# Turning float64 weights into float32 on the chip: another sign operation, one chunk cut in two, two products removed

## The chip, the cores and the metric

The kernel runs on one core of a Trainium2 chip. The metric is the device time of one execution in microseconds (us); the time before is the median of three runs, 744.95 us (744.57 to 745.61). The core has five engines that run their own instruction streams and wait for each other by semaphores: TensorE (PE, with its weight load PEld) multiplies matrices into PSUM, VectorE (DVE) and ScalarE (ACT) do elementwise work, GpSimd (POOL) does some copies, and SyncE (SP) issues DMA transfers. SBUF is the working memory, with 128 partitions.

## The reference

```python
# attention: 8 batches, 8 heads, 576 tokens, head width 64
kv  = einsum('bhsd,bhse->bhde', k, v)
out = einsum('bhsd,bhde->bhse', q, kv)
rms = sqrt(mean(out * out, axis=-1) + 1e-06)
x   = (out / rms * g_norm)          # regrouped to 4608 tokens x 512

# feed-forward: w1, w2 are 512 x 1024, w3 is 1024 x 1024, w_out is 1024 x 512
a = x @ w1
b = x @ w2
h = (a * b) @ w3
result = h @ w_out                  # 4608 x 512
```

The activations q, k, v come as float32. The four weights come as float64, and the chip's engines work on float32, so the kernel first has to turn eight bytes of each weight into four.

## The kernel before, in words

The work has a beginning and nine groups of 512 tokens. In the beginning the product of w3 and w_out is formed once (it depends on no token); afterwards each group of tokens is sent through the attention, the two gates a and b, and that folded matrix. The groups use a scheme with seven products in place of eight (`winograd`, line 709), whose sums are formed by DVE.

**The beginning.** w3 and w_out are cut into eight chunks of 128 columns of w3 (or rows of w_out). A chunk is one raw tile of 128 partitions x 1024 float64 values: 512 of the upper half of w3, then 512 of w_out, half a megabyte each. `load_next` (line 191) loads a chunk by two transfers, chunk 0 by four; there are four raw tiles, so the load of chunk 4 needs the raw tile of chunk 0 to be read out. Then, for each chunk c:

1. `conversion` (line 137) writes the 1024 float32 values to `chunks[:, c]`. It sees each float64 as two 32-bit words, `lo` and `hi`. ACT makes two passes: `low` (line 158), lo scaled by 2^-51 plus 2.0, which gives a number between 2 and 2 + 2^-19 whose last bits are the top bits of lo; and line 160, the absolute value of hi read as a float. DVE makes four steps: line 162 takes the sign bit from hi and puts it into `low`; line 166 clamps the absolute value; line 169 shifts it left by three; line 172 adds the two integers. The `yield`s cut this into ACT's first pass, ACT's second pass, and the DVE steps.
2. `turn_w3` (line 676): PE transposes the chunk's w3 part by four products with the identity (line 680), and ACT copies the result to SBUF (line 685).
3. `fold_chunk` (line 689): four products of 512 columns (line 693) add the chunk's share to the folded matrix. The first three stand before the turn of the next chunk, the fourth behind it.

`begin_next` (line 238) issues ACT's two passes of the next chunk, with a call of `between` between the two passes of every piece where it is given; `end_next` (line 247) issues the DVE steps and the next load. `conversions` (line 222) cuts a chunk into pieces, each a conversion of its own: chunk 0 into 256, 256 and 512 values, chunk 1 into 512 and 512, the others whole. The loop at line 1413 issues, for chunk c: the DVE steps of chunk c, three fold products, the turn of chunk c + 1, the fourth fold product. For c = 0 the turn of chunk 1 is passed as `between` to the conversion of chunk 2, so that ACT's copy of turned chunk 1 stands between ACT's two passes over chunk 2.

`keep_warm(n)` (line 271) issues n products of the identity with itself, which nobody reads. It is called with 14 before anything has landed, with 9 behind the turn of chunk 0, and with 2 behind the fourth fold product of chunk 0.

The upper half of w3 is followed by its lower half (four raw tiles, "b") and by w1 and w2 (eight raw tiles, "w"), converted in the same way: 20 raw tiles in all, the last of them in the first group of tokens, about 84 to 115 us from the start. The scratch `low` lies in a part of `ab` that is not yet in use; odd and even tiles take turns with it.

**Order of the work.** In the beginning the order on DVE, ACT and SP is as written; PE, POOL and SP have a written order throughout. Later a scheduler orders ACT and, in part, DVE by its own costs, so that a changed cost of one step can change the order of others.

Of the kernel before, what the change touches and what calls it, by code (L numbers as in the profile page):

```python
# [12 lines left out]
FP32 = mybir.dt.float32  # L13
U32 = mybir.dt.uint32
U16 = mybir.dt.uint16
I64 = mybir.dt.int64
AF = mybir.ActivationFunctionType
ALU = mybir.AluOpType
# [4 lines left out]
def kernel(  # L23
# [32 lines left out]
    nc = tc.nc  # L56
# [49 lines left out]
    def load_q_left(b):  # L106
# [20 lines left out]
    LEAST, MOST = (  # L127
        float(np.array(bits, np.uint32).view(np.float32)) for bits in (0x38000000, 0x47EFFFFF)
    )

    def scale_by(t, scale, by_scalar):
        if by_scalar:
            nc.scalar.activation(t, t, AF.Copy, scale=scale)
        else:
            nc.vector.tensor_scalar(out=t, in0=t, scalar1=scale, scalar2=None, op0=ALU.mult)

    def conversion(n, dst, raw, cols=slice(0, 1024), scale=None, by_scalar=False):

        dst, raw = (t if len(t.shape) == 3 else t[:, cols] for t in (dst, raw))
        if raw.dtype == FP32:  # L140
            yield
            yield
            nc.vector.tensor_copy(out=dst, in_=raw)
            if scale is not None:
                scale_by(dst, scale, by_scalar)
            return
        words = raw.bitcast(U32).rearrange("p (n w) -> p n w", w=2)
        lo, hi = words[:, :, 0], words[:, :, 1]

        low = ab[n % 2][:, NF // 2:].rearrange("p a i t -> p (a i t)")[:, cols]  # L150
        low_bits = low.bitcast(U32)
        if len(dst.shape) == 3:
            wide = dict(c=dst.shape[1])
            lo, hi, low, low_bits = (
                t.rearrange("p (c n) -> p c n", **wide) for t in (lo, hi, low, low_bits)
            )
        dst_bits = dst.bitcast(U32)
        nc.scalar.activation(low, lo, AF.Copy, scale=2.0 ** -51, bias=2.0)
        yield
        nc.scalar.activation(dst, hi.bitcast(FP32), AF.Abs)  # L160
        yield
        nc.vector.scalar_tensor_tensor(  # L162
            out=low_bits, in0=hi, scalar=0x80000000, in1=low_bits,
            op0=ALU.bitwise_and, op1=ALU.bitwise_or,
        )
        nc.vector.tensor_scalar(
            out=dst, in0=dst, scalar1=LEAST, scalar2=MOST, op0=ALU.max, op1=ALU.min
        )
        nc.vector.tensor_scalar(
            out=dst_bits, in0=dst_bits, scalar1=3, scalar2=None, op0=ALU.logical_shift_left  # L170
        )
        nc.vector.tensor_tensor(out=dst_bits, in0=dst_bits, in1=low_bits, op=ALU.add)  # L172
        yield
        if scale is not None:
            scale_by(dst, scale, by_scalar)
# [10 lines left out]
    raws = []  # L186
# [35 lines left out]
    def conversions(n):  # L222

        what, i = todo[n]
        if what == "w":
            dst = w_sb[:, i].rearrange("p w c f -> p (w c f)")

            return [conversion(n, dst, raws[n], scale=g_col, by_scalar=in_first_group)]
        if what == "b":
            return [conversion(n, chunks[:, 2 * i:2 * i + 2, 0, :], raws[n])]  # L230
        dst = chunks[:, i].rearrange("p w f -> p (w f)")
        cuts = [[0, 256, 512, 1024], [0, 512, 1024], [0, 1024]][min(i, 2)]
        return [conversion(n, dst, raws[n], slice(a, b)) for a, b in zip(cuts, cuts[1:])]

    begun = []
    in_first_group = False

    def begin_next(between=None):
        if len(begun) < len(todo):
            begun.append(conversions(len(begun)))  # L240
            for c in begun[-1]:
                next(c)
                if between is not None:
                    between()
                next(c)

# [24 lines left out]
    def keep_warm(n):  # L271

        t = bank(ps_mm, "mm")
        for _ in range(n):
            nc.tensor.matmul(t[:, 0:P], lhsT=ident, rhs=ident, start=True, stop=True)
# [1114 lines left out]
    with tc.manual_schedule(  # L1390
        engines={mybir.EngineType.DVE, mybir.EngineType.Activation, mybir.EngineType.SP}
    ):
        for _ in range(RAW):
            load_next()
        nc.scalar.activation(const.tile([P, 1], FP32, name="warm"), eps_col, AF.Sqrt)
        g_row = const.tile([1, P], FP32, name="g_row")
        for e in range(2):
            nc.scalar.dma_start(
                out=g_row[:, e * D:(e + 1) * D], in_=g_norm.rearrange("(o d) -> o d", o=1)
            )  # L1400


        keep_warm(14)
        begin_next()
        end_next()
        turn_w3(0, 0)
        keep_warm(9)
        begin_next()

        g_ps = bank(ps_at, "at")[:, 0:1]  # L1410
        nc.tensor.transpose(g_ps, g_row, ident[0:1, 0:1])
        nc.scalar.copy(g_col, g_ps)
        for c in range(KF):

            if c:
                begin_next()
            end_next()
            if c == 4:
                load_four("k", 0, 0)
                load_q(0, 0)  # L1420
            elif c == 5:
                load_four("v", 0, 0)
                load_q(0, 1)
                load_q_left(0)
            fold_chunk(0, c, range(NH - 1))
            if c == 0:
                begin_next(lambda: turn_w3(0, 1))
            else:
                turn_w3(*((0, c + 1) if c + 1 < KF else (1, 0)))
            fold_chunk(0, c, [NH - 1])  # L1430
            if c == 0:
                keep_warm(2)


        first = batch(0)
        first.start()
        BEGIN, PRODUCT = {1: 0, 4: 1}, {2: 0, 5: 1}
        norms = {}
        FIRST = len(converted) + KF - 1
        for c in range(KF):  # L1440
            if c in BEGIN:
                first.begin_q(2 * BEGIN[c], 2 * BEGIN[c] + 1)
                if c == max(BEGIN):
                    x_first = first.x_by_dma(0, nc.scalar.copy)
                    next(x_first)
                    next(x_first)
            if c - 1 in norms:
                all_of(norms[c - 1])
            if c < KF - 2:
                if c < max(BEGIN):  # L1450
                    begin_next()
                if c == max(BEGIN) + 1:
                    all_of(x_first)

                end_next(len(raws) < FIRST)
            elif c == KF - 2:
                run(sum_w(0))
            fold_chunk(1, c, [0])
            if c in BEGIN:
                first.begin_kv(BEGIN[c])  # L1460
                if c == max(BEGIN):
                    load_q_left(1)
            if c + 1 == KF:
                for r in range(2):
                    first.turn(2 + r)
                run(combine_x(0))
                end_next(False)
                for _ in range(3):
                    load_next()
            fold_chunk(1, c, range(1, NH - 1))  # L1470
            if c + 1 < KF:
                turn_w3(1, c + 1)
            if c in (max(BEGIN), KF - 2):
                begin_next()
            fold_chunk(1, c, [NH - 1])
            if c in PRODUCT:
                norms[c] = first.product(PRODUCT[c])
                next(norms[c])
                next(norms[c])
# [8 lines left out]
    for n, T in enumerate(groups):  # L1488
# [8 lines left out]
        def between():  # L1497
            while len(converted) < len(begun):
                with tc.issue_after(copies["u2"][-1].ins):
                    end_next()  # L1500
            next(pieces, lambda: None)()
            if T == FIRST_OF_TWO - 1 and p == 0:
                begun_p.append(True)
                if len(begun_p) == 2:
                    with tc.issue_after(adds["norm"].ins):
                        prepare_some(2)
            if T == FIRST_OF_TWO - 1 and p == 1 and len(prepared) < 3:
                with tc.issue_after(adds["c11" if len(prepared) > 1 else "c21"][-1].ins):
                    prepare_some(1)
            if T == 1 and p == 2 and not loaded_b:  # L1510
                for _ in range(3):
                    load_b()
            if T == FIRST_OF_TWO - 1 and p == 2:
                replaced.append(True)
                if len(replaced) == 2:
                    replace_a21()

        if T in IN_TWO:
            p = 2
# [130 lines left out]
```

## Time and profile before

| | |
|---|---|
| median of three runs | 744.95 us |
| the profiled execution | 744.86 us |
| its span, first to last instruction | 743.0 us |
| PE busy | 736.0 us |
| DVE busy | 629.7 us |
| ACT busy | 378.1 us |
| POOL busy | 21.8 us |
| sign step of the conversion (L162) | 23 instructions, 21.9 us in 18 of 1024 elements |
| products of `keep_warm` (L275) | 50 matrix instructions for 25 products |

One execution is recorded; the times are from the start of its span. "L162" is line 162 of the kernel. A group of the profile lists instructions of one line, engine and shape: their number, their busy time in us and the mean of one in ns, and then how long the engine was idle before them and what ended that. A float32 product shows as two matrix instructions. The chain of waits goes back from the last instruction, at each step to whatever released it; its shares tell which engine sets the time where. An engine can be busy all the time and set nothing, and one that is idle for a microsecond can set everything behind it. The granted clock is the share of TensorE's full clock that it was given.

### The profile page before, as it was taken

How to read it: one execution, taken by the hardware profiler on the slowest of the kernel's cores; microseconds unless marked ns; L12 is line 12 of the kernel's file. 1: busy time of each engine (PE TensorE's matmuls, PEld its weight loads, DVE VectorE, ACT ScalarE, POOL GpSimd, SP SyncE). 2: the span in 40 equal slices, each digit the busy share in tenths (PEclk: the TensorE clock that was granted, in tenths of full speed). 3: DMA queues.
4: the chain of work that ended last, by engine and by line, in shares of the span. 5: the costliest groups of instructions: out<-in, count | busy, mean ns of one | idle time of the engine just before them, and what ended most of it. 6: DMA issues, size and time to landing. Idle time of an engine off the chain costs nothing.

```text
span 743.0 us, 16815 instructions
## 1 busy us (share of the span) xinstructions
PE 736.0 (99%) x6843; PEld 658.6 (89%) x6843; DVE 629.7 (85%) x1233; ACT 378.1 (51%) x652; POOL 21.8 (3%) x29
## 2 busy tenths in 40 slices
PE   8999999999999999999999999999999999999998
PEld 5455788888899999999999999999999999999997
DVE  6987999967869689978996899689969987997797
ACT  6687777424652575257526752576277313212321
POOL 0000000132000000010000001000001000000000
PEclk9999999999999999999999999999999999999999
DMA  9996934599999698869886998598848662565454
GB/s 313 354 330 203 266 108 122 121 326 301 285 311 326 175 275 260 268 157 287 256 263 169 292 263 257 181 284 239 278 101 220 224 209 87 178 218 158 135 198 135
DMA packets 135456, 169.65 MB, mean 228 GB/s; under 512 B 78036, under 2 KB 110804, under 8 KB 135380
## 3 DMA queue, kind: packets, MB, share of 16 engines
q1 hardware_dynamic: 132928, 154.16, 68.8%
q10 hardware_dynamic: 2452, 14.42, 5.6%
q8 instruction: 54, 0.88, 0.5%
q14 instruction: 22, 0.18, 0.1%
HBM read 130.55 MB, written 20.71 MB: 204 GB/s over the span
## 4 chain that ended last, share of the span: by engine, by line
PE 96%; DVE 2%; ACT 1%; DMA 1%; issue 0%; SPq 0%; ACTq 0%
PE mm L723 36%; PE mm L1273 23%; PE mm L1015 21%; PE mm L693 7%; PE at L335 3%; PE at L723 2%; PE mm L413 1%; PE at L413 1%; PE at L680 1%; DMA raw<-in_moe_w_out_dram 1%; PE at L1316 0%; DVE ab L162 0%; PE at L432 0%; DVE c L896 0%; PE at L355 0%
## 5 line engine op out<-in xcount | busy, mean ns | idle before, releaser
L1064 ACT COPY slots<-mm 128x512 f32<-128x512 f32 x88 | 51.6, 586 | 125.9 <-PE mm L1273 83.1
L723 PE MATMUL mm<-xT,w_sb 128*128 128x256 f32 x448 | 102.9, 379 | 0.0
L723 PEld LDWEIGHTS mm<-xT,w_sb 128*128 128x128 f32 x448 | 84.4, 190 | 11.5 <-issue 0.5
L723 PE MATMUL mm<-xc,ws 128*128 128x256 f32 x336 | 76.1, 379 | 0.0
L723 PEld LDWEIGHTS mm<-xc,ws 128*128 128x128 f32 x336 | 63.8, 190 | 8.7
L741 ACT COPY slots<-mm 128x512 f32<-128x512 f32 x59 | 34.6, 586 | 69.1 <-PE mm L723 63.7
L693 PE MATMUL mm<-chunks,ab 128*128 128x512 f32 x128 | 60.7, 605 | 0.9 <-DVE chunks L172 0.9
L1068 DVE TENSOR_TENSOR slots<-mm,slots 128x512 f32<-128x512 f32 x66 | 45.1, 683 | 17.4 <-PE mm L1015 17.3
L1065 ACT COPY slots<-mm 128x384 f32<-128x384 f32 x88 | 42.3, 481 | 25.3 <-PE mm L1273 22.6
L1015 PE MATMUL mm<-ws,w3o_sb 128*128 128x128 f32 x350 | 53.9, 275 | 0.0
L381 DVE TENSOR_REDUCE inv<-sq 128x8 f32<-128x512 f32 (+1 forms) x40 | 24.6, 629 | 29.0 <-ACT sq L380 29.0
L1273 PE MATMUL mm<-w3o_sb,ab 128*128 128x128 f32 x368 | 48.9, 276 | 0.0
L1015 PEld LDWEIGHTS mm<-ws,w3o_sb 128*128 128x128 f32 x350 | 46.4, 192 | 0.0
L1273 PEld LDWEIGHTS mm<-w3o_sb,ab 128*128 128x128 f32 x368 | 45.4, 192 | 0.6
L1273 PE MATMUL mm<-w3o_sb,raw 128*128 128x128 f32 x340 | 43.5, 275 | 0.0
L693 PEld LDWEIGHTS mm<-chunks,ab 128*128 128x128 f32 x128 | 21.6, 190 | 22.6 <-issue 14.3
L1273 PEld LDWEIGHTS mm<-w3o_sb,raw 128*128 128x128 f32 x340 | 40.7, 192 | 0.0
L723 PE MATMUL mm<-xc,w_sb 128*128 128x256 f32 x160 | 38.5, 384 | 0.0
L723 PE MATMUL mm<-xT,ws 128*128 128x256 f32 x160 | 38.2, 382 | 0.1
L1069 DVE TENSOR_TENSOR slots<-mm,slots 128x384 f32<-128x384 f32 x66 | 36.4, 551 | 1.9 <-PE mm L1273 1.9
L308 ACT COPY xT<-xn 128x1024 uint16<-128x1024 uint16 x28 | 32.5, 1167 | 4.3 <-DMA xn<-xT 4.3
L723 PEld LDWEIGHTS mm<-xT,ws 128*128 128x128 f32 x160 | 30.1, 190 | 4.6 <-ACT slots L741 0.5
(243 smaller groups left out, 1649.0 us busy)
## 6 DMA issues: line engine op xcount, KB each, us to landing
w3o_sb<-w_l SPq DMA_DIRECT2D x21, 896.0 KB, 4.7
w3o_sb<-w3o_l SPq DMA_DIRECT2D x18, 896.0 KB, 6.7
raw<-in_moe_w_dram SPq DMA_DIRECT2D x31, 512.0 KB, 7.6
raw<-w3o_l SPq DMA_DIRECT2D x15, 896.0 KB, 4.7
w3o_sb<-w3o_l ACTq DMA_DIRECT2D x14, 896.0 KB, 4.6
k_sb<-in_k_dram SPq DMA_DIRECT2D x16, 576.0 KB, 5.1
v_sb<-in_v_dram SPq DMA_DIRECT2D x16, 576.0 KB, 6.3
q_sb<-in_q_dram SPq DMA_DIRECT2D x32, 256.0 KB, 4.0
```

The costliest lines, as they stand in the source:

```text
L308: copy(words(dst), src)
L335: nc.tensor.matmul(ps[r * D:(r + 1) * D, :], lhsT=k_sb[rows, r, cols], rhs=v_sb[rows, r, cols], start=(j == 0), stop=(j == JS - 1),)
L381: adds["norm"] = nc.vector.tensor_reduce(out=inv[:, i], in_=sq.rearrange("p (h d) -> p h d", d=D), axis=AX.X, op=ALU.add)
L693: nc.tensor.matmul(sums_ps[half][m], lhsT=w3T[half, c][:, m, :], rhs=chunks[:, c, 1, :], start=(c == 0), stop=(c == KF - 1),)
L723: nc.tensor.matmul(ps[:, u, :], lhsT=lhsT(a_name, u, c), rhs=rhs(b_name, c),  start=(u == 0 and c == 0 and new), stop=(c == chunks - 1), s ...
L741: copies.setdefault(name, []).append(nc.scalar.copy(t, ps))
L1015: nc.tensor.matmul(ps[place // 4][:, place % 4, :], lhsT=x, rhs=y, start=new and place // 4 not in seen, stop=True, skip_group_check=True,)
L1064: nc.scalar.copy(z[:, 0:4], ps[0])
L1065: return nc.scalar.copy(z[:, 4:7], ps[1][:, 0:3])
L1068: nc.vector.tensor_add(z[:, 0:4], ps[0], z[:, 0:4])
L1069: nc.vector.tensor_add(z[:, 4:7], ps[1][:, 0:3], z[:, 4:7])
L1273: nc.tensor.matmul(ps[place // 4][:, place % 4, :], lhsT=x[:, c, :], rhs=y[:, c, :], start=new and place // 4 not in seen, stop=(c == 1), ...
```

## The change

Four things are changed in the conversion and in the loop that calls it:

- The sign step has one input in place of two. The upper 16 bits of `low` are the same for every element (0x4000, as `low` lies between 2 and 2 + 2^-19). The new step reads the top 16 bits of each float64 (every fourth 16-bit element of the raw tile), keeps the sign bit, sets 0x4000, and writes the upper 16 bits of each element of `low` (every second 16-bit element).
- The passes and steps are kept in lists, and for the w_out piece of chunk 0 (`low_last`) their order is exchanged: ACT makes the absolute value first and `low` second, and DVE clamps and shifts first and takes the sign third.
- Chunk 2 is converted in two pieces of 512, w3 part and w_out part. `between` is called once per chunk, between the two passes of its last piece.
- The `keep_warm(2)` behind chunk 0 is gone.

```diff
+        low_top = low.bitcast(U16).rearrange("p (n w) -> p n w", w=2)[:, :, 1]
+        hi_top = raw.bitcast(U16).rearrange("p (n w) -> p n w", w=4)[:, :, 3]
...
-        nc.scalar.activation(low, lo, AF.Copy, scale=2.0 ** -51, bias=2.0)
-        yield
-        nc.scalar.activation(dst, hi.bitcast(FP32), AF.Abs)
-        yield
-        nc.vector.scalar_tensor_tensor(
-            out=low_bits, in0=hi, scalar=0x80000000, in1=low_bits,
-            op0=ALU.bitwise_and, op1=ALU.bitwise_or,
-        )
-        nc.vector.tensor_scalar(
-            out=dst, in0=dst, scalar1=LEAST, scalar2=MOST, op0=ALU.max, op1=ALU.min
-        )
-        nc.vector.tensor_scalar(
-            out=dst_bits, in0=dst_bits, scalar1=3, scalar2=None, op0=ALU.logical_shift_left
-        )
+        passes = [
+            lambda: nc.scalar.activation(low, lo, AF.Copy, scale=2.0 ** -51, bias=2.0),
+            lambda: nc.scalar.activation(dst, hi.bitcast(FP32), AF.Abs),
+        ]
+        steps = [
+            lambda: nc.vector.tensor_scalar(
+                out=low_top, in0=hi_top, scalar1=0x8000, scalar2=0x4000,
+                op0=ALU.bitwise_and, op1=ALU.bitwise_or,
+            ),
+            lambda: nc.vector.tensor_scalar(
+                out=dst, in0=dst, scalar1=LEAST, scalar2=MOST, op0=ALU.max, op1=ALU.min
+            ),
+            lambda: nc.vector.tensor_scalar(
+                out=dst_bits, in0=dst_bits, scalar1=3, scalar2=None, op0=ALU.logical_shift_left
+            ),
+        ]
+        if low_last:
+            passes, steps = passes[1:] + passes[:1], steps[1:] + steps[:1]
+        for f in passes:
+            f()
+            yield
+        for f in steps:
+            f()
         nc.vector.tensor_tensor(out=dst_bits, in0=dst_bits, in1=low_bits, op=ALU.add)
...
-        cuts = [[0, 256, 512, 1024], [0, 512, 1024], [0, 1024]][min(i, 2)]
-        return [conversion(n, dst, raws[n], slice(a, b)) for a, b in zip(cuts, cuts[1:])]
+        cuts = [[0, 256, 512, 1024], [0, 512, 1024], [0, 512, 1024], [0, 1024]][min(i, 3)]
+        return [
+            conversion(n, dst, raws[n], slice(a, b), low_last=i == 0 and a == 512)
+            for a, b in zip(cuts, cuts[1:])
+        ]
...
-                if between is not None:
+                if between is not None and c is begun[-1][-1]:
                     between()
...
-            if c == 0:
-                keep_warm(2)
```

## The prediction

> **What bounds the kernel now.** I read the busy shares and the chain on the page first, then the table of windows, then the chain of the first 25 us in order of time, then the rows of ScalarE (ACT) and VectorE (DVE) in those microseconds.
>
> ```profile
> PE 736.0 (99%) x6843; PEld 658.6 (89%) x6843; DVE 629.7 (85%) x1233; ACT 378.1 (51%) x652; POOL 21.8 (3%) x29
> ...
> PE 96%; DVE 2%; ACT 1%; DMA 1%; issue 0%; SPq 0%; ACTq 0%
> ```
>
> TensorE is busy for 736.0 of 743.0 us: only about 7 us in the whole run can be won by feeding it better. The windows say where these are:
>
> ```profile
> 9.00:18.58 9.58, 7.88 (x29) 3.96 (x28) 9.31 (x16) 7.58 (x11) 0.00 (x0) 1.00 1.06 380
> 18.58:42.59 24.01, 24.01 (x73) 11.03 (x74) 23.49 (x26) 16.82 (x20) 0.00 (x0) 1.00 1.05 353
> 83.34:130.00 46.66, 46.58 (x407) 40.42 (x406) 44.16 (x77) 35.73 (x58) 0.00 (x0) 1.00 0.48 133
> 130.00:735.00 605.00, 605.00 (x5875) 570.39 (x5874) 513.39 (x1057) 281.52 (x505) 21.10 (x23) 1.00 0.75 227
> ```
>
> Columns: stretch, length, busy time of PE, PEld, DVE, ACT, POOL, granted clock, DMA share, GB/s. PE misses 1.7 us between 9.00 and 18.58 and next to nothing from 18.58 to 735. What the change can win lies before 18.58, or a little later where new waits would appear. The chain there:
>
> ```profile
> 14.67 1.22 DVE ab L162
> 15.89 0.66 DVE chunks L166
> 16.57 0.70 DVE chunks L169
> 17.30 1.24 DVE chunks L172
> 18.54 0.04 issue
> 18.58 0.66 PE at L680 x4
> 19.24 3.52 PE mm L693 x8
> 22.75 0.44 PE at L680 x4
> ```
>
> The conversion of chunk 2 (four DVE steps of 1024 elements) ends at 18.54 and only then PE may turn it (L680). From there a chunk costs PE 4.00 us (turns of chunks 3, 4 and 5 start at 22.59, 26.55, 30.56) and DVE 3.73 us (L162 at 14.67, 18.44, 22.17), so PE is the bound. Whatever time PE has won at the turn of chunk 3, before 22.59, it keeps to the end, unless a later stage eats it.
>
> **The price of the new sign step.** The groups of the first 24 us:
>
> ```profile
> L162 DVE SCALAR_TENSOR_TENSOR ab<-raw,ab 128x1024 uint32<-128x1024 uint32 x3 | 3.7, 1219 | 0.0
> ...
> L162 DVE SCALAR_TENSOR_TENSOR ab<-raw,ab 128x512 uint32<-128x512 uint32 x3 | 2.1, 687 | 1.2 <-ACT ab L158 1.2
> L169 DVE TENSOR_SCALAR chunks<-chunks 128x1024 uint32<-128x1024 uint32 x2 | 1.4, 694 | 0.1
> L169 DVE TENSOR_SCALAR chunks<-chunks 128x512 uint32<-128x512 uint32 x3 | 1.3, 427 | 0.1
> ```
>
> The new step has one input, as L169 has: 0.69 us for 1024 elements and 0.43 for 512, against 1.22 and 0.69 of L162. It writes 2-byte elements with a gap, which no DVE row shows. Lower end 0.43 for 1024 (as if it ran like L169 at half the elements); upper end 1.22 (no gain over L162, which reads the same strided source). ACT's 16-bit strided copies (L294, L308: 1.05 to 1.18 us for 1024) cost no more than its 32-bit passes L158 and L160 (1.14 to 1.21), so the gap alone is no expense there. I take 0.69 and 0.43: same engine, same operation class, same count.
>
> The Trainium skill, VectorE: DVE Perf Modes, "What auto-detection actually checks", gives a one-source operation in SBUF two elements per cycle even with steps, and the fourfold rate only for 16-bit data of step 1; the trace shows the twofold rate at L169 alone. Against the change speaks Vector Engine (DVE) Microarchitecture Reference, "Measured stream behaviour on trn2": a port that hops every element costs 1.7 to 2.5 ns per column. By that an estimate is 1.0 to 1.4 us per 1024 (512 columns a port, 0.15 us fixed), and the sum below would become about 0.4 us won to 0.9 us lost; L162's source hops too and its 1219 ns equal L172's 1226 for the same words in one run, so at one element per cycle this trace shows no such cost.
>
> **The change step by step.** Pitches on DVE (start to start, same rows): a 512-step is followed after 0.45 us by one that needs its result and after its duration less 0.08 by one that does not (L162 at 10.41, L166 at 11.02); for 1024: 0.73 and duration less 0.09.
>
> 1. *Exchanged passes, chunk 0's w_out piece.* Its data come at 7.57 as now. Abs runs first, so the clamp starts at 8.28, shift 8.73, sign 9.07 (the low pass ends at 8.82), add 9.52 in place of 9.80. The first fold product moves from 10.64 to 10.36. Were the sign at its upper end, the add would start at 9.78: the exchange alone wins next to nothing.
>
> 2. *Chunk 1.* Two pieces of 0.34 + 0.45 + 0.46 + 0.61 = 1.86 in place of 2.13: DVE goes on at 13.86 in place of 14.67.
>
> 3. *Two unread products fewer.* They stand at 14.59, in PE's wait for ACT's copy of turned chunk 1 (14.13 to 14.72 now; 13.85 to 14.44 after, as its turn moves with the first product). Chunk 1's fold starts at about 14.60 in place of 15.04: 0.28 is step 1, 0.16 the products. PE then waits 0.27 us, less than the 0.89 and 0.80 it waits at 10.64 and 18.58 under a granted clock of 1.00, so I price the clock at nothing.
>
> 4. *Chunk 2 in two pieces.* DVE pays one set of fixed costs more (2 x 1.86 = 3.72, against 3.31 for one of 1024 with the new sign), but the turn needs the first piece alone, done at 15.80. PE turns chunk 2 after its three products, at 17.25 in place of 18.58. The second piece is done at 17.66. On ACT the first piece goes at 11.62 into idle time (idle from 11.61 to 13.05; chunk 2's w3 half has landed by then, as 1.4 us pass between landings), the second at 13.05; the copy of turned chunk 1 keeps its place before the last pass.
>
> 5. *What is late next: chunk 3.* Its data bound ACT, not the sign:
>
> ```profile
> 13.05 1.20 ACT L158 ACTIVATE ab<-raw 128x1024 f32<-128x1024 uint32 x1 [1.44 <-DMA raw<-in_moe_w_out_dram]
> 14.13 0.59 ACT L685 COPY ab<-at 128x512 f32<-128x512 f32 x1
> ...
> 15.84 1.17 ACT L158 ACTIVATE ab<-raw 128x1024 f32<-128x1024 uint32 x1
> 16.91 1.14 ACT L160 ACTIVATE chunks<-raw 128x1024 f32<-128x1024 f32 x1
> ```
>
> The trace's landing of chunk 3's last half is 15.73, so ACT's two passes cannot move and end at 18.05. The copy of turned chunk 2 comes behind them, 18.0 to 18.58, and chunk 2's fold can start at about 18.75, PE's own pace giving 18.62: 0.12 lost. DVE: sign of chunk 3 at 17.58, clamp 18.18 (it waits for ACT's 18.05), add 19.63, end 20.86. PE turns chunk 3 at about 21.35 in place of 22.59: **1.24 us won**, and DVE is half a microsecond ahead.
>
> 6. *Afterwards.* A chunk costs DVE about 3.2 us, PE 4.00; chunk 4 lands at 18.5 by the trace, ACT takes it up at 18.6 (19.75 now), chunk 5 at 21.3. DMA is full (share 1.05) but gains 1.2 us per chunk on PE. The load of chunk 4 is the one that waits for the sign's read: issued at 9.04 now, about 9.6 after, behind queues that are full until 15.73; nothing waits on SP's queue but the later loads. From 18.58 to 735 PE has no wait worth naming, except 0.24 us near 128.1 behind ACT's copy L741, whose row of ACT work starts from PE itself at 114.19 and moves with it. Some thirteen later signs save DVE 0.53 each; PE doesn't wait for them. The scheduler exchanges a few steps between 94 and 115 us: on ACT a scaling (L133, 1.14 us) gets ahead of a copy of a product (98.97); its bank is held until DVE's L896 at 106.00 in either case. Price nothing; if one such bank were awaited, 1.1 us.
>
> The sum: 744.86 of the profiled execution (span 743.0 and 1.86 around it) less 1.24 is 743.62; the median is 0.09 above that execution, so 743.7.
>
> **The rivals.**
> - *The sign gains nothing* (1.22 for 1024). Adds then end at 10.47, 14.73, 18.99 and 22.73 for chunks 0 to 3: chunk 2 in two pieces costs DVE 0.53, PE turns chunk 3 at 22.77. 0.18 lost: 745.1. For it: no such DVE row; against: L169. Between 0.82 and 1.22 the result slides from 743.7 to 745.1.
> - *More is won*: the wait near 128.1 (0.24) vanishes as DVE is relieved in 83 to 130 (44.16 of 46.66 busy): 743.4. Against: that chain is ACT's. A still faster sign wins nothing, because of chunk 3's landing.
> - *Slower*: the 2-byte gapped write costs DVE more than L162. Place: the seven half-steps up to chunk 3's add, then every chunk. From about 1.55 us for 1024 the run is slower by over 0.2%: the seven halves add 1.15 to the 0.18, and DVE's chunk exceeds PE's 4.00 from 1.49 on. At twice L162's price: 4.3 us by chunk 3, then six conversions at 0.95 each, some 755. Against: ACT's strided rows.
> - *A later bank wait* (step 6) takes 1.1 back: 744.8.
>
> **How the numbers follow.** Forecast 0.74, no gain in the sign 0.11, more won 0.07, slower 0.05, later wait 0.03. About 0.2% (1.5 us) is what a measurement of this kernel can tell from no change. The three runs before spread 1.04 us, so the forecast's own range is 743.2 to 744.2; a fifth of it, and most of "more won", lies under 743.46: faster 0.20; slower the 0.05 and a stray of the no-gain case, 0.07; same 0.73. The range takes in the sliding sign price: 743.1 to 745.2.
>
> **What would show it.** The new DVE step at 0.69 (1024) and 0.43 (512); first fold product near 10.4; turn of chunk 2 near 17.3, of chunk 3 near 21.4, both without a wait for DVE; ACT's first pass of chunk 3 still at 15.84; PE busy about as before in a span of 741.8. Wrong would make it: a sign above 0.82, a landing of chunk 3 that moves, or a PE wait after 22 us that isn't in this trace.

## The result and the profile after

The changed kernel takes 743.12 us (median of 14 runs, 742.60 to 745.01) against 744.98 us for the kernel before (14 runs, 744.24 to 745.61): a ratio of 0.9978, 95% interval 0.9970 to 0.9985. The gain is 1.86 us, 0.25%, just over the 0.2% that can be told from no change. The forecast was 743.7, with 743.1 to 745.2 as its range and most of the chance on "within 0.2%": the direction was right, the size was forecast 0.6 us too small, and 743.12 lies just inside the lower end of the range.

The profiled execution of the changed kernel took 742.95 us with a span of 741.0, 2.0 less than before. In its code the lines have moved: the sign is L166 (was L162), the clamp L170 (L166), the shift L173 (L169), the addition L184 (L172), ACT's two passes L162 and L163 (L158, L160), the turn L695 (L680), ACT's copy of the turned chunk L700 (L685), the fold L708 (L693), and in the later stages L738 was L723 and L756 was L741.

The busy shares and the shares of the chain, from the page:

```profile
PE 735.2 (99%) x6839; PEld 658.3 (89%) x6839; DVE 622.0 (84%) x1237; ACT 379.0 (51%) x654; POOL 21.9 (3%) x29
...
PE 97%; DMA 2%; ACT 0%; SPq 0%; issue 0%; DVE 0%; ACTq 0%
```

PE is busy for 0.8 us less, in part because it makes two products fewer, so most of the 2.0 us is idle time that is gone. DVE, which held 2% of the chain before, has left it. The table of windows, with the columns that the prediction explains; the first stretch ends behind the turn of chunk 2, which starts at 16.93:

```profile
9.00:17.40 8.40, 7.56 (x26) 3.63 (x25) 8.09 (x18) 7.08 (x13) 0.00 (x0) 1.00 1.06 383
17.40:41.40 24.00, 23.80 (x74) 10.86 (x73) 21.50 (x28) 17.88 (x22) 0.00 (x0) 1.00 1.08 362
82.00:128.70 46.70, 46.70 (x408) 40.77 (x407) 41.85 (x77) 35.95 (x58) 0.00 (x0) 1.00 0.47 130
```

PE now misses 0.84 us in the first stretch in place of 1.70, and 0.20 in the second, where before it missed nothing. DVE has 2.5 us to spare in the second stretch (0.5 before). The chain in the first 22 us, in order of time, shows what ends last there:

```profile
7.05 8.68 DMA raw<-in_moe_w_out_dram
...
15.83 1.17 ACT ab L162
16.99 0.60 ACT chunks L163
17.59 0.35 issue
17.94 0.60 ACT ab L700
18.55 0.04 issue
18.59 2.84 PE mm L708 x6
```

Where four DVE steps stood, there is now the landing of chunk 3 at 15.72, ACT's two passes over it, and the copy of turned chunk 2. The groups of DVE by shape in the first 24 us, the new sign with the clamp beside it:

```profile
L166 DVE TENSOR_SCALAR ab<-raw 128x512 uint16<-128x512 uint16 x5 | 2.3, 455 | 0.0
L166 DVE TENSOR_SCALAR ab<-raw 128x1024 uint16<-128x1024 uint16 x3 | 2.3, 753 | 0.0
...
L170 DVE TENSOR_SCALAR chunks<-chunks 128x1024 f32<-128x1024 f32 x2 | 1.4, 688 | 0.0
```

The sign costs 0.753 us for 1024 elements and 0.455 for 512, against 1.219 and 0.687 before. And PE's own timeline, with the waits in brackets:

```profile
10.19 2.81 PE L708 MATMUL mm<-chunks,ab 128*128 128x512 f32 x6 [0.84 <-ACT chunks L163]
...
16.93 0.60 PE L695 MATMUL at<-ident,chunks 128*128 128x128 f32 x4
...
18.59 2.84 PE L708 MATMUL mm<-chunks,ab 128*128 128x512 f32 x6 [0.20 <-ACT ab L700]
21.27 0.60 PE L695 MATMUL at<-ident,chunks 128*128 128x128 f32 x4
```

Chunk 2 is turned at 16.93 (18.58 before) without a wait, and chunk 3 at 21.27 (22.59). When the same PE instructions of both traces are laid side by side, the changed kernel is ahead by 1.65 us at the turn of chunk 2, 1.32 at the turn of chunk 3, 1.57 at 54 us, 1.60 from 66 to 128 us, 1.92 from 129 us on, and 2.0 at the end. So there are three places: the start (1.32), the pace of the following chunks (0.28), and one place near 128 us (0.32). There PE's weight loads wait for a copy of ACT, first in the kernel before, then in the changed one:

```profile
128.60 1.38 PEld L723 LDWEIGHTS mm<-xT,ws 128*128 128x128 f32 x7 [0.48 <-ACT slots L741]
...
126.68 1.59 PEld L738 LDWEIGHTS mm<-xT,ws 128*128 128x128 f32 x8 [0.17 <-ACT slots L756]
```

### The profile page after: what moved, and what is told of

It is laid out like the page before. It is cut to its first block, busy times and chain, and to the rows that moved or that the text cites. A ratio compares the mean times of both kernels' runs of the same rounds, so it can differ in the third digit from the quotient of the medians.

```text
span 741.0 us, 16817 instructions
## 1 busy us (share of the span) xinstructions
PE 735.2 (99%) x6839; PEld 658.3 (89%) x6839; DVE 622.0 (84%) x1237; ACT 379.0 (51%) x654; POOL 21.9 (3%) x29
## 4 chain that ended last, share of the span: by engine, by line
PE 97%; DMA 2%; ACT 0%; SPq 0%; issue 0%; DVE 0%; ACTq 0%
PE mm L738 38%; PE mm L1288 23%; PE mm L1030 21%; PE mm L708 7%; PE at L350 3%; PE at L738 2%; DMA raw<-in_moe_w_out_dram 2%; PE mm L428 1%; PE at L428 1%; PE at L695 1%; PE at L1331 0%; PE at L447 0%; PE at L370 0%; SPq L210 0%; ACT ab L162 0%; PE at L464 0%
## 5 line engine op out<-in xcount | busy, mean ns | idle before, releaser
L738 PE MATMUL mm<-xT,w_sb 128*128 128x256 f32 x448 | 102.9, 379 | 0.0
L738 PEld LDWEIGHTS mm<-xT,w_sb 128*128 128x128 f32 x448 | 84.4, 190 | 11.5 <-issue 0.5
L738 PE MATMUL mm<-xc,ws 128*128 128x256 f32 x336 | 76.1, 379 | 0.0
L738 PEld LDWEIGHTS mm<-xc,ws 128*128 128x128 f32 x336 | 63.8, 190 | 8.7
L756 ACT COPY slots<-mm 128x512 f32<-128x512 f32 x59 | 34.6, 587 | 68.9 <-PE mm L738 63.8
L708 PE MATMUL mm<-chunks,ab 128*128 128x512 f32 x128 | 60.7, 605 | 1.0 <-ACT chunks L163 0.8
L708 PEld LDWEIGHTS mm<-chunks,ab 128*128 128x128 f32 x128 | 21.6, 190 | 23.4 <-issue 14.4
L738 PE MATMUL mm<-xc,w_sb 128*128 128x256 f32 x160 | 38.5, 384 | 0.0
L738 PE MATMUL mm<-xT,ws 128*128 128x256 f32 x160 | 38.1, 381 | 0.0
L738 PEld LDWEIGHTS mm<-xT,ws 128*128 128x128 f32 x160 | 30.1, 190 | 4.3 <-ACT slots L756 0.2
```

Source lines behind the costliest of these rows:

```text
L708: nc.tensor.matmul(sums_ps[half][m], lhsT=w3T[half, c][:, m, :], rhs=chunks[:, c, 1, :], start=(c == 0), stop=(c == KF - 1),)
L738: nc.tensor.matmul(ps[:, u, :], lhsT=lhsT(a_name, u, c), rhs=rhs(b_name, c),  start=(u == 0 and c == 0 and new), stop=(c == chunks - 1), s ...
L756: copies.setdefault(name, []).append(nc.scalar.copy(t, ps))
```

## The experiments

The theory was the prediction's: the start is won by chunk 2's pieces and the cheap sign together, and what ends last afterwards is chunk 3's landing on ACT. The rivals were that one part alone brings the gain, that the sign itself still sets the pace, and, for the place near 128 us, that the cheaper late signs remove the wait there.

Single executions differ in when the first weights land (chunk 0's last transfer between about 6.5 and 7.9 us), so the table also gives the turn of chunk 3 as a distance from the landing of chunk 3's last half in the same execution. The pace is the mean distance from one turn to the next from chunk 4 to chunk 7. The last column is what PE's weight loads wait near 128 us for ACT's copy to `slots`. The last two rows are single executions of the two kernels.

| kernel | median us | ratio (95% interval) | turn of chunk 2 | turn of chunk 3 | chunk 3 landed | distance | pace | wait |
|---|---|---|---|---|---|---|---|---|
| before | 744.98 | 1 | 18.58 | 22.59 | 15.73 | 6.86 | 4.01 | 0.48 |
| after | 743.12 | 0.9978 (0.9970 to 0.9985) | 16.93 | 21.27 | 15.72 | 5.55 | 3.955 | 0.17 |
| sign alone | 744.21 | 0.9985 (0.9976 to 0.9994) | 18.49 | 22.50 | 15.71 | 6.79 | 3.955 | 0.16 |
| all but the sign | 744.55 | 0.9993 (0.9984 to 1.0002) | 17.04 | 22.28 | 15.23 | 7.05 | 4.01 | 0.19 |
| old sign for w1, w2 | 743.03 | 0.9977 (0.9969 to 0.9986) | 16.96 | 21.22 | 15.69 | 5.53 | 3.955 | 0.20 |
| two products back | 743.12 | 0.9976 (0.9966 to 0.9986) | 17.43 | 21.38 | 15.84 | 5.54 | 3.955 | 0.16 |
| chunk 2 whole | 744.49 | 0.9995 (0.9986 to 1.0003) | 18.32 | 22.30 | 15.42 | 6.88 | 3.955 | 0.16 |
| no sign, chunks 0 to 3 | 742.73 | 0.9966 (0.9954 to 0.9978) | 16.62 | 20.94 | 15.44 | 5.50 | 3.955 | 0.17 |
| chunk 3 in two | 742.74 | 0.9970 (0.9958 to 0.9982) | 16.70 | 20.66 | 15.43 | 5.23 | 3.955 | 0.17 |
| chunk 0 finer too | 742.29 | 0.9961 (0.9949 to 0.9973) | 16.71 | 20.66 | 15.50 | 5.16 | 3.955 | 0.16 |
| before, other execution | 745.33 | | 18.98 | 22.99 | 16.13 | 6.86 | 4.01 | 0.52 |
| after, other execution | 743.12 | | 17.24 | 21.47 | 15.93 | 5.54 | 3.955 | 0.16 |

The kernel before had a median of 744.92 us beside the experiments from "sign alone" to "two products back" and 745.02 beside those from "chunk 2 whole" to "chunk 0 finer too"; each ratio is to the kernel before that ran beside it. Beside the last two rows, one more execution of the kernel before took 746.17.

**The sign alone.** The kernel before with only the sign step replaced, which is the changed kernel with the rest undone:

```diff
-        cuts = [[0, 256, 512, 1024], [0, 512, 1024], [0, 512, 1024], [0, 1024]][min(i, 3)]
+        cuts = [[0, 256, 512, 1024], [0, 512, 1024], [0, 1024]][min(i, 2)]
...
-            conversion(n, dst, raws[n], slice(a, b), low_last=i == 0 and a == 512)
+            conversion(n, dst, raws[n], slice(a, b), low_last=False)
...
-                if between is not None and c is begun[-1][-1]:
+                if between is not None:
...
+            if c == 0:
+                keep_warm(2)
```

> The kernel before with the new sign step alone: chunk 2 whole, passes of chunk 0 in the old order, the two products there. The theory: nothing is won at the beginning, since VectorE's clamp of chunk 2 started at 15.84 in the profile of before, right behind ScalarE's absolute value (14.60 to 15.81), so a shorter sign in front of it only waits longer: the turn of chunk 2 stays at 18.5 to 18.6, that of chunk 3 at 22.5 to 22.6. Late, near 128 us, the wait of 0.46 us between two products is gone, as in the changed kernel: 744.98 less 0.35 to 0.5, so 744.5 to 744.7. The rival, that the cheaper sign itself gives the gain (each of five half-steps and one whole step before chunk 3 is 0.24 to 0.47 us shorter): turn of chunk 2 near 17.8, of chunk 3 near 21.7, and 743.7 or less.

It took 744.21, 0.7 less than the kernel before. DVE's timeline:

```profile
14.24 0.76 DVE L166 TENSOR_SCALAR ab<-raw 128x1024 uint16<-128x1024 uint16 x1 [0.30 <-ACT ab L162]
15.76 0.69 DVE L170 TENSOR_SCALAR chunks<-chunks 128x1024 f32<-128x1024 f32 x1 [0.76 <-ACT chunks L163]
```

The sign gave DVE its time back and DVE then stood still: it waits 0.30 us for ACT's first pass over chunk 2 and 0.76 us for the second. Chunk 2 is turned at 18.49, only 0.09 earlier than before. PE is still 0.09 ahead at the turn of chunk 3, 0.39 at 66 us (the quicker pace), and 0.71 from 129 us on, where the long wait of before is absent; that is the 0.7 of the median. So nearly none of the sign's own gain lies at the start.

**All but the sign.** The changed kernel with the old sign step in its place:

```diff
-            lambda: nc.vector.tensor_scalar(
-                out=low_top, in0=hi_top, scalar1=0x8000, scalar2=0x4000,
+            lambda: nc.vector.scalar_tensor_tensor(
+                out=low_bits, in0=hi, scalar=0x80000000, in1=low_bits,
                 op0=ALU.bitwise_and, op1=ALU.bitwise_or,
             ),
```

> The changed kernel with the old two-input sign step (1.22 us for 1024): chunk 2 in two pieces, passes exchanged, two products fewer. The prediction's rival worked this out: VectorE pays 0.53 us more for chunk 2 and PE turns chunk 3 at about 22.7, 0.2 later than before; turn of chunk 2 at about 17.5, then a wait of the fold of chunk 2 for its second piece (done near 19.0). The wait near 128 us comes back. 745.0 to 745.2, so no gain is left. The rival, that the split of chunk 2 gives the gain by itself: turn of chunk 3 at 21.4 to 21.6 and 743.3 to 743.8.

It took 744.55; the interval of the ratio holds 1. PE's timeline:

```profile
17.04 0.60 PE L695 MATMUL at<-ident,chunks 128*128 128x128 f32 x4
...
22.28 0.65 PE L695 MATMUL at<-ident,chunks 128*128 128x128 f32 x4 [0.82 <-DVE chunks L184]
```

Chunk 2 is turned 1.5 us earlier than in the kernel before, 0.5 of which comes with data that landed 0.5 us earlier in this execution (chunk 0 and chunk 3 alike). At chunk 3 the rest is lost again: PE waits 0.82 us for DVE, which has one set of fixed costs more to pay and no cheaper sign to pay it with. The distance from the landing is 7.05 against 6.86, so the start is 0.19 us worse than before. The prediction's rival without a gain in the sign had worked out 0.18. The long wait near 128 us did not come back (0.19), though all signs are the old ones.

**Chunk 2 whole.** The changed kernel without the split:

```diff
-        cuts = [[0, 256, 512, 1024], [0, 512, 1024], [0, 512, 1024], [0, 1024]][min(i, 3)]
+        cuts = [[0, 256, 512, 1024], [0, 512, 1024], [0, 1024]][min(i, 2)]
```

> The changed kernel with chunk 2 converted whole again. The theory that the split is what opens the way and the cheaper sign what makes it affordable: ScalarE's absolute value of chunk 2 ends near 15.7 again, VectorE's clamp waits for it, the turn of chunk 2 is at 18.4 to 18.5 and that of chunk 3 at 22.4 to 22.5, as with the sign alone (744.21): 744.1 to 744.4. The rival, that the parts add up and the split is one of several equal shares: turn of chunk 3 near 21.7, 743.5.

It took 744.49 against 745.02 for the kernel before; the interval of the ratio holds 1. DVE's timeline has the same wait as with the sign alone:

```profile
15.49 0.69 DVE L170 TENSOR_SCALAR chunks<-chunks 128x1024 f32<-128x1024 f32 x1 [0.79 <-ACT chunks L163]
```

The turn of chunk 3 stands 6.88 us behind the landing, as before (6.86). With the cheap sign, the exchanged order and the products removed, the start gains nothing while chunk 2 is whole: ACT's second pass of 1024 elements ends at 15.46, and DVE cannot pass it.

**Two products back.** The changed kernel with the two unread products in their old place:

```diff
             fold_chunk(0, c, [NH - 1])
+            if c == 0:
+                keep_warm(2)
```

> The changed kernel with the two unread products back behind chunk 0's fold. The prediction gave them 0.16 us. The profile of the changed kernel says less: the fold of chunk 2 waits for ScalarE's copy of turned chunk 2 (17.94 to 18.53), which stands behind ScalarE's passes over chunk 3, whose data land at 15.72. The turn of chunk 2 comes 0.1 to 0.2 later (17.1), its copy still at 17.94, the turn of chunk 3 still at 21.3: 743.1. If the products do cost, as the prediction has it, the turn of chunk 3 is at 21.45 and the time 743.3.

743.12, the same median as without them. Chunk 2 was turned at 17.43, half a microsecond later than in the changed kernel (chunk 0 had also landed 0.27 later), but chunk 3 at the same distance from its landing, 5.54. What the products cost lies ahead of a wait and is swallowed by it.

**The late signs.** The changed kernel with the old sign step for the eight raw tiles of w1 and w2 only, which are converted up to 115 us:

```diff
-            lambda: nc.vector.tensor_scalar(
+            (lambda: nc.vector.scalar_tensor_tensor(
+                out=low_bits, in0=hi, scalar=0x80000000, in1=low_bits,
+                op0=ALU.bitwise_and, op1=ALU.bitwise_or,
+            )) if todo[n][0] == "w" else (lambda: nc.vector.tensor_scalar(
                 out=low_top, in0=hi_top, scalar1=0x8000, scalar2=0x4000,
                 op0=ALU.bitwise_and, op1=ALU.bitwise_or,
-            ),
+            )),
```

> The changed kernel, with the old sign step in the eight raw tiles of w1 and w2 alone; all tiles of w3 and w_out keep the new one. The theory that the new sign also removed the wait near 128 us: it is back, a pause of 0.4 to 0.5 us between two products of line 738, everything before about 45 us is as in the changed kernel (turn of chunk 3 at 21.2 to 21.4), and the time is 743.12 plus 0.3 to 0.4, so 743.4 to 743.5. The rival, that the wait near 128 us comes and goes by chance or by the earlier start: it stays away, 743.1.

743.03. The long wait near 128 us did not come back (0.20), so my explanation, that cheaper late signs had removed it, fell.

**What sets the turn of chunk 3 in the changed kernel.** The sign step is left out for chunks 0 to 3:

```diff
+        if todo[n][0] == "c" and todo[n][1] < 4:
+            steps = [s for i, s in enumerate(steps) if i != (2 if low_last else 0)]
```

> The changed kernel with the sign step left out for chunks 0 to 3 (the signs of those weights are lost): VectorE's work on them is 0.24 to 0.6 us shorter per piece. The theory that ScalarE's passes over chunk 3, whose data land at 15.7, and the copy behind them are now the bound: ScalarE's first pass of chunk 3 at 15.8, the copy of turned chunk 2 at 17.9, turn of chunk 3 at 21.2 to 21.3, 743.0 to 743.2. The rival, that VectorE's sign is still on the path: turn of chunk 3 at 20.9 or earlier, 742.7 or less.

742.73. That is less than was expected, and the turn of chunk 3 at 20.94 lies near the rival's 20.9, so the timelines have to decide. ACT's timeline, and then PE's:

```profile
15.55 1.15 ACT L162 ACTIVATE ab<-raw 128x1024 f32<-128x1024 uint32 x1 [1.08 <-DMA raw<-in_moe_w_out_dram]
...
17.64 0.57 ACT L702 COPY ab<-at 128x512 f32<-128x512 f32 x1
```

```profile
18.27 2.84 PE L710 MATMUL mm<-chunks,ab 128*128 128x512 f32 x6 [0.19 <-ACT ab L702]
20.94 0.60 PE L697 MATMUL at<-ident,chunks 128*128 128x128 f32 x4
```

With no sign at all, ACT's first pass over chunk 3 still waits for the landing, PE waits for the copy behind ACT's passes, and chunk 3 is turned 5.50 us behind its landing (5.55 with the sign). The 0.33 us that PE is ahead of the changed kernel at this turn comes with a landing that was 0.28 earlier in this execution. That accounts for the profile, and speaks for the landing and against the sign; why the median of the five runs is 0.4 lower than the changed kernel's stays open.

**Chunk 3 in two pieces.** If chunk 3's passes on ACT hold the copy of turned chunk 2 up, shorter passes must help:

```diff
-        cuts = [[0, 256, 512, 1024], [0, 512, 1024], [0, 512, 1024], [0, 1024]][min(i, 3)]
+        cuts = [[0, 256, 512, 1024], [0, 512, 1024], [0, 512, 1024], [0, 512, 1024], [0, 1024]][min(i, 4)]
```

> The changed kernel with chunk 3 in two pieces as well: ScalarE takes the w3 half (landed at 14.4) at 14.8, the w_out half at 16.0 and is done at 17.25, so that the copy of turned chunk 2 starts at 17.55 with no wait. The theory of ScalarE as the bound: fold of chunk 2 starts at 18.25 in place of 18.59, turn of chunk 3 at 20.9 to 21.0, and 743.12 less 0.35, so 742.75. The rival, that VectorE's 0.5 us more for chunk 3 eat it: turn of chunk 3 as now, 743.1 or more.

742.74. ACT's timeline:

```profile
17.34 0.59 ACT L700 COPY ab<-at 128x512 f32<-128x512 f32 x1 [0.51 <-PE at L695]
```

The copy now waits for PE, not PE for the copy; chunk 3 is turned at 20.66, 3.96 us behind chunk 2 (the pace of the chunks that follow), where the changed kernel needed 4.34. The bound that was named is the bound. The profile shows this and the median does not: the kernel without the early signs, in which the copy still waits, has the same median (742.73).

**Chunk 0's w_out piece cut as well.** Two pieces of 256, both in the exchanged order (the edit is against the kernel just above):

```diff
-        cuts = [[0, 256, 512, 1024], [0, 512, 1024], [0, 512, 1024], [0, 512, 1024], [0, 1024]][min(i, 4)]
+        cuts = [[0, 256, 512, 768, 1024], [0, 512, 1024], [0, 512, 1024], [0, 512, 1024], [0, 1024]][min(i, 4)]
...
-            conversion(n, dst, raws[n], slice(a, b), low_last=i == 0 and a == 512)
+            conversion(n, dst, raws[n], slice(a, b), low_last=i == 0 and a >= 512)
```

> As e8, and chunk 0's w_out part in two pieces of 256 with the exchanged order in both, so that ScalarE begins with the first half when it lands (6.6) and not with the second (7.3). First fold product near 9.7 in place of 10.19, turn of chunk 2 near 16.5, its copy near 17.25 behind ScalarE's passes, turn of chunk 3 near 20.5: 0.7 to 0.8 below the changed kernel, 742.3 to 742.5. The rival, that VectorE's fixed costs of one piece more take it back: turn of chunk 3 as in e8, 742.75.

742.29, the fastest kernel of this study and 0.39% under the kernel before (0.27% to 0.51%). But the start gives no reason for it: the first fold product begins at 9.91 (10.19 in the changed kernel), and the turns of chunks 2 and 3 stand where chunk 3 in two pieces had put them, 16.71 and 20.66. ACT's timeline shows what holds the gain back:

```profile
12.82 0.69 ACT L162 ACTIVATE ab<-raw 128x512 f32<-128x512 uint32 x1
13.40 0.58 ACT L700 COPY ab<-at 128x512 f32<-128x512 f32 x1
```

The copy of turned chunk 1 stands behind the first pass over chunk 2's second piece, and that waits for its landing at 12.71. Whether the 0.45 us between these two kernels' medians, of five runs each, has to do with the edit is open.

**Both kernels once more.** A second execution of the kernel before and of the changed kernel.

> The kernel before, another execution. The wait of 0.46 us between two products near 128.1 us was there in the profile of before and in none of the six kernels looked at since, two of which keep the old sign late. Theory: it is no property of the old sign step but of one execution or of its phase; then it is missing here, the row of PE instructions differs from the profile of before by the landing of chunk 0 alone at first (turn of chunk 3 at 22.3 to 22.6), and falls 0.3 us behind nothing at 128. The rival, that the kernel before always has it: a gap of 0.4 to 0.5 us between two products at 127.8 to 128.2.

> The changed kernel, another execution: turn of chunk 3 at 21.0 to 21.4, set by ScalarE's passes over chunk 3, whatever the landing of chunk 0 (6.9 to 7.5); no wait near 126 us. If the start were still set by chunk 0's landing, the turn of chunk 3 would move with it by the same time.

PE's timeline in the changed kernel:

```profile
17.24 0.60 PE L695 MATMUL at<-ident,chunks 128*128 128x128 f32 x4
...
21.47 0.60 PE L695 MATMUL at<-ident,chunks 128*128 128x128 f32 x4
```

Chunk 0 landed 0.44 us later than in the first execution, chunk 3 0.21 later; chunk 3 was turned 0.20 later, at 21.47, just behind the 21.4 that was expected. It goes with chunk 3's landing, not with chunk 0's. In the kernel before, chunk 0 landed 0.45 and chunk 3 0.40 later and the turn came 0.40 later, which does not tell the two apart.

The second execution of the kernel before has the long wait near 128 us too (0.52), so, against what was expected, it is no chance of a single execution. The chain of the kernel before leads up to it so:

```profile
124.39 0.70 DVE c L896
125.08 0.02 issue
125.10 0.04 ACTq L741
125.14 0.32 issue
125.46 0.04 ACT inner_sums L741
...
128.06 0.49 ACT slots L741
```

and this is ACT's timeline with all but the sign changed:

```profile
124.90 0.58 ACT L756 COPY inner_sums<-mm 128x512 f32<-128x512 f32 x1 [1.19 <-PE mm L738]
```

ACT's queue had its signal for this copy at 125.10 before and at 124.82 in the other kernel, where all neighbouring instructions are also 0.28 earlier. But the copy itself starts 0.36 us behind the signal before (in both executions) and 0.08 in the other; in the ten rows that are not the kernel before it is 0.08 to 0.14. This 0.28 us is what PE's wait at 128.6 is longer by (0.48 against 0.19). Both executions of the kernel before have a wait of 0.48 to 0.52 us and the other ten rows of the table 0.16 to 0.20, with the new sign or with the old one. Nothing that the profile shows is awaited in those 0.32 us of "issue". The cause is not settled; what is shown is that the long wait is absent with the new sign alone and with the rest of the change alone as well.

**The pace of the chunks.** The same traces show where the 0.055 us per chunk come from. These are the copies of turned chunks in the kernel before, and then in the changed kernel:

```profile
L685 ACT COPY ab<-at x16: 567/586/618, 8.7 to 78.1; 128x512 f32<-128x512 f32 x16
L685 ACTq EVENT_SEMAPHORE  x9: 17/17/17, 27.2 to 62.6; - x9
```

```profile
L700 ACT COPY ab<-at x16: 563/586/638, 8.5 to 76.5; 128x512 f32<-128x512 f32 x16
```

In the kernel before, nine of the copies, from chunk 4 on, have an instruction of their own in front that only waits for PE's semaphore. Such a copy starts 0.69 us behind the start of its turn (27.24 behind 26.55), one without it 0.64 us (23.23 behind 22.59 at chunk 3 of the same kernel, 29.82 behind 29.18 in the changed one), and the fold products that need the copy come later by about the same time. So in the kernel before chunk 4 is turned 3.96 us behind chunk 3, and only the chunks after it need 4.01. The three traces with the old sign in the chunks (both of the kernel before, and all but the sign) have nine of these instructions each; the other nine traces have none. Why the old sign step brings these instructions into the program was not tried.

The exchanged order of chunk 0's passes was not tried alone. With chunk 2 whole and the new sign, the exchange and the removal of the two products together bring the start nothing (a distance of 6.88 with both, 6.79 in the kernel with the sign alone).

## Why the prediction was right, and where it was not

- **The bound** was right in the main (for the 0.055 us per chunk that it leaves out see step 6). After the change PE is again busy without a gap from chunk 3 on, and what the start won was kept to the end: PE was never less ahead than the 1.32 us at the turn of chunk 3.
- **The price of the sign** was a little low: 0.753 us measured against the 0.69 taken, and 0.455 against 0.43, nearest to the row it was taken from and under the 0.82 from which it would have mattered. The Trainium skill, VectorE: DVE Perf Modes, "What auto-detection actually checks", lets a one-source operation in SBUF do two elements per cycle with steps; that agrees with 0.753 us beside 0.688 for the clamp L170, whose elements lie side by side. Vector Engine (DVE) Microarchitecture Reference, "Measured stream behaviour on trn2", gives 1.7 to 2.5 ns per column for a port that hops every element, from which the prediction had made an estimate of 1.0 to 1.4 us; the rows here show no such cost at these steps, only 0.065 us.
- **Step 1** gave 10.36 for the first fold product; it came at 10.19. The execution's data had landed 0.22 us earlier (7.26 against 7.48), which explains the difference and a little more. **Step 2**, DVE going on to chunk 2 at 13.86, came as 13.69, early by the same 0.17.
- **Step 3** put 0.16 us on the two unread products. With them back chunk 2 is turned later (17.43), but the time and the distance at chunk 3 are the same: the 0.16 lies ahead of the wait that step 5 names. The prediction's own sum had swallowed it too: without the 0.16, PE's pace would have brought chunk 2's fold to 18.78, beside the 18.75 that the copy sets. As far as these runs can tell, removing the products was no part of the gain.
- **Step 4** had the turn of chunk 2 at 17.25; it came at 16.93 (17.24 in the second execution). The reason given, that the turn needs the first piece alone, is only half of it: with chunk 2 whole, DVE's clamp waits 0.76 to 0.79 us for ACT's second pass of 1024 elements. The split shortens that pass too, and without this the cheaper sign bought the start next to nothing (0.09 us). The prediction did not look at it.
- **Step 5** was right in mechanism and size. Chunk 3's landing and ACT's first pass at 15.83 (forecast 15.84) did not move; the copy of turned chunk 2 stood at 17.94 to 18.53 (18.0 to 18.58), the fold at 18.59 (18.75), the turn at 21.27 (21.35). 1.32 us were won against 1.24. That a still faster sign wins nothing held when the sign was left out: 5.50 us behind the landing against 5.55.
- **Step 6** is where the number failed: "from 18.58 to 735" nothing was to be won. The chunks' pace on PE fell from 4.01 to 3.955 us wherever the new sign was in (eight kernels) and stayed at 4.01 where it was not (two kernels), 0.28 us in all. The step took PE's pace as fixed by PE alone because the windows showed it full; the pace took in the copy of the turned chunk, which in the kernel before stood behind an instruction more. And of the wait near 128.1 the step said that its row of ACT work starts from PE and moves with it. The chain shows that it runs through DVE L896 and a stretch of "issue" on ACT that none of the other kernels has; 0.32 us went there. Neither gain was foreseen; that the time, with them, still lies 0.02 us inside the range is luck.
- **The sum**: 1.24 forecast for the profiled execution, 0.08 more at the start, 0.28 of pace, 0.32 near 128 and 0.08 behind it make the 2.0 us of the span.
- **The rivals.** "More is won" at 743.4 named the place near 128 us, but for a reason (DVE relieved) that the old signs disprove. "The sign gains nothing" was not the case; its working was borne out by the kernel with the old sign (0.19 lost at chunk 3 against 0.18), though that kernel is at 744.55 and not 745.1; the long wait near 128 us, which went there too, accounts for 0.29 of that. No slower sign and no new bank wait showed.
- **The chances.** A ratio of 0.9978 falls into the "faster" that was given 0.20, and not into the "same" with 0.73, though its interval reaches over the border of 0.998. The parts do not add up: the sign alone brings 0.7 us, the rest without the sign 0.4 and all but the split 0.5 (neither of these two clear of noise), all together 1.86. The 1.3 us at the start need the split and the cheap sign together; the prediction's working has that, and its likeliest case was too small in the main by what lies behind the start.

## What to carry to other kernels

Before pricing a cheaper step, look at what the step behind it waits for: here a DVE step that became 0.47 us shorter gave the start 0.09 us by itself, as DVE then stood waiting for ACT. A finer cut and a cheaper step can each be worth nothing and together more than a microsecond, the cut because it lets the next engine begin on half, the cheap step because it pays for the cut's second set of fixed costs. When a start has been tightened, compare executions in which two landings moved by different times: the one with which the work moves is the bound, and the next gain lies behind it (here chunk 3's landing and the passes over it, 0.3 us). An engine that is busy without a gap can still be paced by another: read the instructions around its hand-overs.

## What the runs showed that was not expected

A DVE operation on 16-bit halves, reading every fourth and writing every second element, took 0.753 us for 1024 and 0.455 for 512 elements, 0.065 and 0.041 over a 32-bit operation on adjacent elements (0.688 and 0.414).

The first weights land at different times in different executions: chunk 0's last transfer between 6.5 and 7.9 us, chunk 3's between 15.2 and 16.1 us. A comparison of two single traces at the start is worth no more than some 0.5 us until that is taken out. Later on, a single execution can lose time by itself: the profiled one with the sign alone lost 1.9 us between 222 and 236 us, with PE waiting 1.0 us of it for a transfer:

```profile
PE mm L1288 <- DMA w3o_sb<-w3o_l: 1.0, 2, 0.6
```

The columns are the total wait in us, the number of waits and the longest. Its own time was 746.24, while the median of its 11 runs is 744.21.

An instruction on ACT that only waits, in front of a copy, put the copy 0.055 us later, and PE's pace per chunk went from 3.955 to 4.01 us with it.

ACT started one copy 0.36 us behind its signal in the kernel before and 0.08 behind in the kernel with all but the sign, with the same neighbours and the same instruction ahead. The profile names nothing for it.
